# Moving two projection products, two reductions and an output gating in a fused attention and MLP kernel

## The chip, the cores and the metric

The kernel runs on one core of a Trainium2 chip. The metric is the device time of one execution in microseconds (us), as a median of several runs. A core has engines that run side by side, each through its own list of instructions in order: PE (TensorE, matrix products), DVE (VectorE), ACT (ScalarE), POOL (GpSimd) and SP (SyncE, which here issues most DMAs). They wait for one another by semaphores.

## What is computed

```python
x = A_x
xn = _layernorm(x, axis=-1)
s = _A_ref(xn, A_k_cache, A_v_cache, A_wq, A_wo)   # softmax attention, 32 heads of 128, 2048 queries, 2048 keys, then @ wo
g = _silu(_B_ref(xn, B_w1, B_w2, B_w3, B_w4))      # a token-shifted mixer and a gelu MLP of width 1792
return x + s * g
```

The model width is 512 and all tensors are bf16.

## The kernel before, in words

**Stages.** A first part computes the layer norms and the B branch up to the gate; what is left of the B branch runs beside the first units of attention. Attention is the main loop. A *unit* `u` is one head times 512 queries; there are 128, ordered by groups of four heads (`g`), query tile (`qt`), head (`hh`). A unit has eight *slots* (`SPU`), and `n` counts slots over the whole loop, `p` within the unit. In each slot PE makes two score matmuls (`s_slot`, tile `ps_s`, 128x512 each), ACT takes the exponential of both at once (L447, tile `pT`), and PE makes two probability times value matmuls (`pv_slot`, tile `ps_o`) for the slot ten back. The score tile has two buffers in PSUM, so a slot's score matmuls wait for the exponential of the slot two back.

**Sums of the softmax.** DVE and POOL add up a unit's exponentials: `add_first` (L453), `add_half` (L458, one half on POOL, one on DVE), `add_next` (L462). `fold` (L466) and `fold_last` (L470) halve the result twice. `turn` (L495) sends it through a DMA transpose into `tT`, issued by SP; `turned_sums` (L500) reduces it on DVE, a reciprocal follows, and two DMAs (`dr`, then `rb`, `bcast`, L512) spread it over the partitions. `norm` (L524) multiplies the unit's output by it into `oT`.

**Query projection.** For most units the queries of two heads at a time are made by a seven-product scheme (Strassen with shared sums): `product(v, k)`, k from 1 to 7, two matmuls of 128x256 each into `ps_q`; `q_take` (L416, ACT) and `q_part` (DVE: part 0 is L424, part 1 L427, part 2 L429, part 3 L432) add the products up. The sixteen slots of units v-2 and v-1 are the pair's schedule: product 1 in slot 0, 6 in 2, 2 in 5, 7 in 8, 5 in 9, 4 in 12 and 3 in 13. Parts 0 to 3 run in slots 2, 9, 9 and 14; the score matmuls of unit v start in slot 16 and read what part 3 writes.

**Output projection.** The product with `wo` has the same seven-product form in most (g, qt) blocks: `wo_product` (two matmuls of 128x256 into `ps_wo`), `wo_take` (L598, DVE, adds a product into the running output `sacc`), `o_sum` (L573, DVE, builds the sums of `oT` in the buffers so0 to so3, one buffer each). A block has two rounds `i` of sixteen slots; in round i product k stands in slots 10, 11, 14, 15, 19, 20 and 23 for k = 1, 7, 2, 4, 6, 5, 3, and takes in 12, 16, 22 and 24. `o_sum` 0 of the next block comes in slot 4 of that block, which is slot 20 of the last round of the one before, and it overwrites so0, which product 5 of that round reads. In the other blocks (the first and the last ones) plain matmuls of 128x512 are spread over the slots, each followed by an addition on DVE (L657, L664 or L668).

**The output.** For the first eight token tiles the last stage is `y_last`: a gating multiplication (L676), an addition of the residual (L678) and a DMA out. One tile becomes ready in each of the last units, in slot 7, and `y_last` runs in slot 3 of the next unit. For the other tiles the gate is applied ahead of time (`y_scale`, L636, and the residual by `y_add`, L640). The loads of the residual and the gate use a pool of six buffers.

**Order.** The order on each engine is that of the program: it is written out by hand, slot by slot, in the tables `steps`, `o_steps` and `o_early` and in the main loop at the end. All matmuls have the line of one helper, L112, so they are told apart by their tiles: `ps_s`, `ps_o`, `ps_q`, `ps_wo`.

Of the kernel before, what the change touches and what calls it, by code (L numbers as in the profile page):

```python
# [9 lines left out]
ALU = mybir.AluOpType  # L10
# [7 lines left out]
def kernel(  # L18
# [15 lines left out]
    nc = tc.nc  # L34
# [16 lines left out]
    HG = 4  # L51
# [10 lines left out]
    pin = tc.keep_in_program_order  # L62
# [48 lines left out]
    def mm(out, lhsT, rhs, start, stop, **kw):  # L111
# [9 lines left out]
        out=ident[:], in0=diag[:], scalar1=0.0, scalar2=None, op0=ALU.is_equal))  # L121
# [276 lines left out]
    def turned(v, ps):  # L398
        return ps.rearrange("d i (r j) -> d i j r", j=4) if v in TURN else ps.unsqueeze(2)

    def q_tile(v, pl, **kw):
        shape = [P, 4, 4, 64] if v in TURN else [P, 4, 1, 256]
        return pl.tile(shape if "bufs" not in kw else [P] + shape[2:], **kw)
# [14 lines left out]
    def q_part(v, i):  # L418
        s = sw[v]
        ps = turned(v, s["ps"][:])  # L420
        t = lambda: q_tile(v, pS, dtype=FP32, tag="tq", bufs=3, name="tq")
        if i == 0:
            s["u"] = t()
            pin(nc.vector.tensor_tensor(out=s["u"][:], in0=ps[:, 1], in1=s["m1"][:], op=ALU.add))  # L424
        elif i == 1:
            s["u3"] = t()
            pin(nc.vector.tensor_tensor(out=s["u3"][:], in0=ps[:, 0], in1=s["u"][:], op=ALU.add))  # L427
        elif i == 2:
            pin(nc.vector.tensor_tensor(out=s["q"][:, 3], in0=ps[:, 1], in1=s["u3"][:], op=ALU.add))  # L429
        else:  # L430
            u = s["u"][:].unsqueeze(1)
            pin(nc.vector.tensor_tensor(  # L432
                out=s["q"][:, 1:3], in0=ps, in1=u.to_broadcast([P, 2] + list(u.shape[2:])), op=ALU.add))
            del sw[v]
# [33 lines left out]
    def fold_last(u):  # L468
        a = st[u]["acc"]
        pin(nc.vector.tensor_tensor(out=a[:, 0, :], in0=a[:, 0, :], in1=a[:, 1, :], op=ALU.add))  # L470
# [56 lines left out]
    sacc = {}  # L527
# [8 lines left out]
    def halves(x):  # L536
        return x.rearrange("p (a c) -> p a c", a=2)
# [74 lines left out]
    wog, sp, tw, so, wo_ps, gin = {}, {}, {}, {}, {}, {}  # L612
# [56 lines left out]
        if g == NG - 1:  # L669
            last.append(t)  # L670

    pair, last = {}, deque()

    def y_last(t):
        xl, gl = fin.pop(t), gin[t]
        pin(nc.vector.scalar_tensor_tensor(  # L676
            out=halves(gl), in0=sacc[t], scalar=0.5, in1=halves(gl), op0=ALU.mult, op1=ALU.mult))
        pin(nc.vector.tensor_tensor(out=xl[:], in0=gl, in1=xl[:], op=ALU.add))  # L678
        pin(nc.sync.dma_start(out=out2d[t * P:(t + 1) * P, :], in_=xl[:]))

# [314 lines left out]
    for g in range(NG - 1):  # L995
        b = (g * QT + QT - 1) * HG
        for hh in range(HG):
            h = (g + 1) * HG + hh
# [32 lines left out]
    def pv_run(n):  # L1031
        while pv_at[0] <= n - LAG:
            pv_slot(*divmod(pv_at[0], SPU))
            pv_at[0] += 1
# [11 lines left out]
    def wo_slot(part, n, each=2, **kw):  # L1046
        gg, t = wo_todo[0]
        if part < HG // each:
            wo_mm(gg, t, tuple(range(part * each, (part + 1) * each)), **kw)
            return  # L1050
        wo_todo.popleft()
        wo_post(gg, t, n)
        if gg == NG - 1 and t % 4 < 3 and t + 1 not in fin and t // 4 not in LATE:
            fin_load(t + 1)
# [7 lines left out]
    first, third = {}, {}  # L1062
    for v in pairs:
        a = (v - 2) * SPU
        for k, n in ((1, 0), (6, 2), (2, 5), (7, 8), (5, 9), (4, 12), (3, 13)):
            steps[a + n].append((product, v, k))
        for i, n in enumerate((0, 5)):
            steps[a + n].append((q_take, v, i))
        steps[a + 14].append((q_part, v, 3))
        first[v - 2] = v  # L1070
        third[v - 1] = (v,)

    o_steps, o_early = defaultdict(list), defaultdict(list)
    for g, qt in BLOCK:
        u0 = ((g * QT + qt) * HG + 6) * SPU
        for i in range(2):
            a = u0 + 16 * i
            for k, n in ((1, 10), (7, 11), (2, 14), (4, 15), (6, 19), (5, 20), (3, 23)):
                steps[a + n].append((wo_product, g, qt, i, k))
            for k, n, which in ((7, 12, o_early), (4, 16, o_early), (5, 22, o_steps), (3, 24, o_early)):  # L1080
                which[a + n].append((wo_take, g, qt, i, k))
        for i, n, which in ((2, 3, o_steps), (0, 4, o_early), (1, 12, o_early), (3, 19, o_steps)):
            which[u0 + n].append((o_sum, g, qt, i))
# [11 lines left out]
    for i, u in enumerate((10, 11, 12, 13, 14, 16, 18, 20)):  # L1095
        n = (LATER + u) * SPU
        t = 4 * LATE[0] + i
# [22 lines left out]
    def run_all(plan, n):  # L1120
        for fn, *args in plan.get(n, ()):
            fn(*args)
# [1 line left out]
    for j, u in enumerate((2, 2, 3, 4, 4, 5, 5, 6, 9, 9, 9, 9, 11, 11, 17, 21)):  # L1124
        at(u * SPU + 3, lambda qt=(j // 4 - 1) % QT, i=j % 4: x_sum(qt, i))
    for h in range(2, H, 2):
        for i, u in enumerate((((-4, -4, -3, -3), (-2, -1, 0, 0))[h % HG // 2] if h >= HG else (8, 8, 9, 9))):
            o_early[(h // HG * QT * HG + u) * SPU + 4].append((w_sum, h, i))

    for v in range(1, NU):  # L1130
# [4 lines left out]
    for n in range(UB * SPU):  # L1135
        u, p = divmod(n, SPU)
        if p == 0 and wo_box and u not in PLAN:
            wo_slot(4, n, each=1)
        s_slot(u, p)
        pv_run(n)  # L1140
        for v, dcs in q_plan.get(n, ()):
            q_mm(v, dcs)
        run_steps(n, product)
        run_steps(n, wo_product)
        run_steps(n, q_take)
        if p == 0 and 1 <= u:
            if u - 2 in TURN:
                turned_sums(u - 2)
                turned_recip(u - 2)
            run_all(o_early, n)  # L1150
            if u not in third:
                add_last(u - 1)
        if p == 1 and u - 2 in TURN:
            bcast(u - 2)
        if p == fold_at(u) and 1 <= u:
            for v in third.get(u, ()):
                add_last(u - 1)
                q_part(v, 1)
                q_part(v, 2)
            fold(u - 1)  # L1160
            if u != UA and u not in first:
                fold_last(u - 1)
        if p == 2 and u in first:
            q_part(first[u], 0)
            fold_last(u - 1)
        if p == 3 and u - 1 in TURN:
            turn(u - 1)
        for part, tag in CATCH.get(n, ()):
            wo_slot(part, n, tag=tag)
        for v, k in ((u + 1, 3), (u + 2, 7)):  # L1170
            if p == k and "psq" in st.get(v, ()) and (k == 3) == (v > FIRST):
                q_copy(v)
        if u - 2 in TURN:
            norm_p, sum_p, wo_p, each = 7, 5, 3, 1
        else:
            norm_p, sum_p, wo_p, each = 4, 5, 4, 1
        at_wo = [wo_p + i for i in range(HG // each + 1)]
        if FIRST - 2 <= u < LAST:
            at_wo = ([1, 3, 4, 6, 7], [0, 2, 3, 6, 7])[u % 2]
        if p == norm_p and 2 <= u and not u - 2 in TURN:  # L1180
            norm_queue(u - 2)
        if p == sum_p and 1 <= u and u - 1 not in TURN:
            sums(u - 1)
        if p == sum_p + 1 and 1 <= u and u - 1 not in TURN:
            bcast(u - 1)
        if u == UA and p in (1, 2, 3):
            wo_slot(p - 1, n)
            if p == 3:
                fold_last(u - 1)
        for at_p, part in PLAN.get(u, ()):  # L1190
            if at_p == p:
                wo_slot(part, n, each=2)
        if p in at_wo and u not in PLAN and wo_todo and pS is not None and (p == at_wo[0] or wo_box):
            wo_slot(at_wo.index(p), n, each=each)
        if p == norm_p and u - 2 in TURN:
            norm_queue(u - 2)
        run_steps(n, q_part)
        if p == 4:
            run_all(o_early, n)
            add_first(u)  # L1200
        run_all(o_steps, n)
        if p == 3 and last:
            y_last(last.popleft())
        if p == 6:
            add_half(u, nc.gpsimd, LO) if u in APART else add_next(u, 2)
        pay()
        held_mm(n)
        for fn in todo.pop(n, ()):
            fn()
        if pS is None and not held:  # L1210
            right.close()
            pS = right.enter_context(pool("pS", side="right", reuse_waits="tile"))
            for tag, n in [("tw0", 2)] + [(x, 1) for x in ("tw1", "tw3", "so0", "so1", "so2", "so3")]:
                pS.tile([P, 2, D // 2], BF16, tag=tag, bufs=n, name="room")
            pS.tile([P, 2, 256], BF16, tag="xs", bufs=XS, name="room")
            pS.tile([P, 256], FP32, tag="tq", bufs=3, name="room")
# [3 lines left out]
    n = UB * SPU  # L1220
# [27 lines left out]
    def pv_to(k):  # L1248
# [29 lines left out]
        out=diag[:], in0=diag[:], scalar1=0.0, scalar2=None, op0=ALU.is_equal))  # L1278
# [98 lines left out]
```

## Time and profile before

| what | value |
|---|---|
| time, median of 3 runs | 1220.84 us (1220.69 to 1221.07) |
| the profiled execution's own time | 1223.74 us |
| span of the profile, first to last instruction | 1221.9 us |
| PE / ACT / DVE / POOL busy | 1208.6 / 1107.4 / 1090.2 / 299.5 us |
| granted TensorE clock | 1.00 |

The profile is of one execution. Busy time of PE is that of matmuls, which are pipelined: a 128x512 matmul is recorded as 0.38 us, and the next one starts 0.216 us after it. A row of the timeline gives the start, the length, engine, line, operation, the tiles, the shape, the count of merged instructions, and in brackets the engine's idle time before it with what ended it. Some matmul records are missing.

### The profile page before, as it was taken

To read this page: it belongs to the slowest core of one execution; us is meant where nothing else is said; L and a number is where in the kernel's file an instruction comes from. 1 tells how busy PE (TensorE), PEld (TensorE's weight loads), DVE (VectorE), ACT (ScalarE), POOL (GpSimd) and SP (SyncE) were. 2 spreads that over 40 slices of the span, in tenths; PEclk is the share of its full clock that TensorE was granted. 3 is DMA by queue.
4 is the path that set the end of the run, shared out by engine and by line. 5 is a ranking of instruction groups with operands and counts; after the bars stand their busy time and mean duration, and the time that the engine had idled before them with its cause. 6 is when DMAs were issued, how large, how long until landed. Compare 5 with 4: busy or idle time off the path is not lost.

```text
span 1221.9 us, 18835 instructions
## 1 busy us (share of the span) xinstructions
PE 1208.6 (99%) x6534; PEld 673.1 (55%) x6657; DVE 1090.2 (89%) x1931; ACT 1107.4 (91%) x1243; POOL 299.5 (25%) x222
## 2 busy tenths in 40 slices
PE   9999999999999999999999999999999999999998
PEld 6466444555555555555555555555555555555455
DVE  7863788999999989999999899999999999989997
ACT  6345999999999999999999999999999999999996
POOL 5300001323222222222222222222222222223320
PEclk9999999999999999999999999999999999999999
DMA  7672323434443434345345434343443534356642
GB/s 178 170 154 57 56 57 83 96 90 94 82 86 84 104 61 96 82 96 91 71 90 87 100 69 85 90 96 78 87 87 87 100 72 89 83 107 108 119 113 66
DMA packets 248159, 113.07 MB, mean 93 GB/s; under 512 B 195328, under 2 KB 231296, under 8 KB 248064
## 3 DMA queue, kind: packets, MB, share of 16 engines
q1 hardware_dynamic: 244560, 107.21, 42.2%
q0 software_dynamic: 2944, 4.20, 1.5%
q8 instruction: 52, 0.85, 0.3%
q14 instruction: 43, 0.35, 0.2%
q10 hardware_dynamic: 560, 0.46, 0.1%
HBM read 69.60 MB, written 4.45 MB: 61 GB/s over the span
## 4 chain that ended last, share of the span: by engine, by line
PE 85%; DVE 7%; DMA 5%; issue 1%; ACT 1%; DVEq 0%; POOL 0%
PE ps_s L112 36%; PE ps_o L112 32%; PE ps_q L112 7%; PE ps_wo L112 7%; PE ps_m L112 3%; DMA tT<-acc 2%; DMA rb<-dr 2%; DVE acc L462 1%; ACT pT L447 1%; DVE sm L500 1%; DMA dr<-rc 1%; DVE acc L453 1%; DVE acc L458 1%; DVE oT L524 0%; DVE acc L466 0%
## 5 line engine op out<-in xcount | busy, mean ns | idle before, releaser
L447 ACT ACTIVATE pT<-ps_s 128x1024 bf16<-128x1024 f32 x1016 | 1016.4, 1028 | 45.4 <-PE ps_s L112 14.3
L112 PE MATMUL ps_s<-qT,kT 128*128 128x512 bf16 (+1 forms) x2056 | 607.5, 377 | 1.0 <-DVE qT L432 0.7
L112 PE MATMUL ps_o<-pT,vb 128*128 128x512 bf16 x1884 | 568.3, 379 | 4.7
L458 POOL TENSOR_TENSOR acc<-acc,pT 128x1024 bf16<-128x1024 bf16 x117 | 248.7, 2126 | 726.6 <-DVE acc L453 448.8
L112 PEld LDWEIGHTS <-vb 128*128 128x128 bf16 x1984 | 194.0, 98 | 216.6
L112 PEld LDWEIGHTS <-kT 128*128 128x128 bf16 x2064 | 230.8, 113 | 73.0 <-DVE qT L432 2.4
L462 DVE TENSOR_TENSOR acc<-acc,pT 128x2048 bf16<-128x2048 bf16 x137 | 167.7, 1224 | 20.9 <-ACT pT L447 5.1
L453 DVE TENSOR_TENSOR acc<-pT 128x2048 bf16<-128x2048 bf16 x127 | 154.7, 1218 | 9.2 <-ACT pT L447 9.1
L598 DVE TENSOR_TENSOR sacc<-ps_wo,sacc 128x512 f32<-128x512 f32 x200 | 121.9, 609 | 3.4 <-PE ps_wo L112 1.8
L524 DVE TENSOR_TENSOR oT<-ps_o,rb 128x512 bf16<-128x512 f32 x127 | 86.5, 681 | 8.8 <-DMA rb<-dr 8.4
L500 DVE TENSOR_REDUCE sm<-tT 128x4 f32<-128x512 bf16 x124 | 83.9, 676 | 7.6 <-DMA tT<-acc 7.3
L466 DVE TENSOR_TENSOR acc<-acc 128x1024 bf16<-128x1024 bf16 x127 | 87.2, 687 | 2.4
L458 DVE TENSOR_TENSOR acc<-acc,pT 128x1024 bf16<-128x1024 bf16 x117 | 80.1, 684 | 0.0
L112 PEld LDWEIGHTS <-wc 128*128 128x128 bf16 x448 | 43.8, 98 | 53.3 <-issue 0.7
L112 PE MATMUL ps_wo<-wo_h,oT 128*128 128x256 bf16 (+1 forms) x294 | 70.7, 307 | 0.5
L112 PEld LDWEIGHTS <-oT 128*128 128x128 bf16 x428 | 41.6, 98 | 45.6
L112 PEld LDWEIGHTS <-so 128*128 128x128 bf16 x400 | 39.1, 98 | 48.2 <-issue 1.3
L112 PEld LDWEIGHTS <-wq_h 128*128 128x128 bf16 x396 | 38.7, 98 | 46.0
L112 PE MATMUL ps_q<-xnT,wq_h 128*128 128x256 bf16 (+1 forms) x281 | 58.2, 294 | 0.2
L301 ACT ACTIVATE h2T<-ps_s 128x1024 bf16<-128x1024 f32 x28 | 28.7, 1023 | 31.6 <-PE ps_s L112 31.6
L470 DVE TENSOR_TENSOR acc<-acc 128x512 bf16<-128x512 bf16 x127 | 53.4, 420 | 2.4
L112 PEld LDWEIGHTS <-w_sb 128*128 128x128 bf16 x368 | 33.5, 98 | 29.2
(134 smaller groups left out, 923.6 us busy)
## 6 DMA issues: line engine op xcount, KB each, us to landing
rb<-dr SPq DMA_DIRECT2D x127, 256.0 KB, 4.0
vb<-in_A_v_cache_dram SPq DMA_DIRECT2D x62, 256.0 KB, 3.0
wq_h<-in_A_wq_dram SPq DMA_DIRECT2D x32, 128.0 KB, 2.5
wo_h<-in_A_wo_dram SPq DMA_DIRECT2D x32, 128.0 KB, 2.6
w_sb<-in_B_w_dram SPq DMA_DIRECT2D x8, 256.0 KB, 4.9
kT<-in_A_k_cache_dram SPq DMA_TRANSPOSE x128, 2.7
gate<-xall POOLq DMA_DIRECT2D x16, 128.0 KB, 2.4
sacc<-in_A_x_dram POOLq DMA_DIRECT2D x8, 256.0 KB, 4.5
```

The costliest lines, as they stand in the source:

```text
L112: pin(nc.tensor.matmul(out=out, lhsT=lhsT, rhs=rhs, start=start, stop=stop, **kw))
L301: pin(nc.scalar.activation(out=h2[c][:, f], in_=ps[:], func=ACT.Gelu_apprx_tanh))
L447: pin(nc.scalar.activation(out=s["pT"][-1][:, jj:jj + 2, :], in_=sps[:], func=ACT.Exp, scale=SCALE))
L453: pin(nc.vector.tensor_tensor(out=s["acc"][:], in0=s["pT"][0][:], in1=s["pT"][1][:], op=ALU.add))
L458: pin(eng.tensor_tensor(out=a[:, part, :], in0=a[:, part, :], in1=e[:, part, :], op=ALU.add))
L462: pin(nc.vector.tensor_tensor(out=a[:], in0=a[:], in1=st[u]["pT"][i][:], op=ALU.add))
L466: pin(nc.vector.tensor_tensor(out=a[:, 0:2, :], in0=a[:, 0:2, :], in1=a[:, 2:4, :], op=ALU.add))
L470: pin(nc.vector.tensor_tensor(out=a[:, 0, :], in0=a[:, 0, :], in1=a[:, 1, :], op=ALU.add))
L500: pin(nc.vector.tensor_reduce(out=sm[:], in_=s["tT"][:], axis=mybir.AxisListType.X, op=ALU.add))
L524: pin(nc.vector.tensor_tensor(out=to, in0=o, in1=rb, op=ALU.mult))
L598: pin(nc.vector.tensor_tensor(out=out, in0=ps, in1=out, op=ALU.add))
```

## The change

It moves work within the hand-written order; nothing is added or left out of the computation.

1. The sixth and fifth output projection products go from slots 19 and 20 of their round to 18 and 19.
2. The fourth query product goes from slot 12 to slot 13 of its pair, where the third stands already.
3. In the first unit of a pair, `fold_last` goes ahead of `q_part` 0; in the second unit, `fold` and `fold_last` go ahead of `q_part` 2.
4. `y_last` loses its gating multiplication, which becomes `y_gate`. A tile that became ready before an odd unit is gated in slot 6 of it, and its addition and DMA follow in slot 3 of the next, even unit; in slot 3 of an even unit the tile that became ready just before is gated and finished as well.
5. One weight sum (`w_sum` 1) of the first head pair of the second group goes one unit later.

```diff
+    pair, last, gated = {}, deque(), []
+
+    def y_gate(t):
+        gl = gin[t]
+        pin(nc.vector.scalar_tensor_tensor(
+            out=halves(gl), in0=sacc[t], scalar=0.5, in1=halves(gl), op0=ALU.mult, op1=ALU.mult))
 
     def y_last(t):
         xl, gl = fin.pop(t), gin[t]
-        pin(nc.vector.scalar_tensor_tensor(
-            out=halves(gl), in0=sacc[t], scalar=0.5, in1=halves(gl), op0=ALU.mult, op1=ALU.mult))
         pin(nc.vector.tensor_tensor(out=xl[:], in0=gl, in1=xl[:], op=ALU.add))
...
-        for k, n in ((1, 0), (6, 2), (2, 5), (7, 8), (5, 9), (4, 12), (3, 13)):
+        for k, n in ((1, 0), (6, 2), (2, 5), (7, 8), (5, 9), (4, 13), (3, 13)):
             steps[a + n].append((product, v, k))
...
-            for k, n in ((1, 10), (7, 11), (2, 14), (4, 15), (6, 19), (5, 20), (3, 23)):
+            for k, n in ((1, 10), (7, 11), (2, 14), (4, 15), (6, 18), (5, 19), (3, 23)):
                 steps[a + n].append((wo_product, g, qt, i, k))
...
-        for i, u in enumerate((((-4, -4, -3, -3), (-2, -1, 0, 0))[h % HG // 2] if h >= HG else (8, 8, 9, 9))):
+        for i, u in enumerate((((-4, -4 if h > HG else -3, -3, -3), (-2, -1, 0, 0))[h % HG // 2] if h >= HG else (8, 8, 9, 9))):
...
             for v in third.get(u, ()):
                 add_last(u - 1)
                 q_part(v, 1)
-                q_part(v, 2)
             fold(u - 1)
             if u != UA and u not in first:
                 fold_last(u - 1)
+            for v in third.get(u, ()):
+                q_part(v, 2)
         if p == 2 and u in first:
+            fold_last(u - 1)
             q_part(first[u], 0)
-            fold_last(u - 1)
...
-        if p == 3 and last:
-            y_last(last.popleft())
+        if p == 3 and u % 2 == 0:
+            if gated:
+                y_last(gated.pop())
+            if last:
+                y_gate(last[0])
+                y_last(last.popleft())
+        if p == 6 and u % 2 and last:
+            y_gate(last[0])
+            gated.append(last.popleft())
```

More of the change, by code (lines that the diff above doesn't have):

```diff
@@ L670, in wo_post @@
             last.append(t)
-    pair, last = {}, deque()
+    pair, last, gated = {}, deque(), []
[3 more added lines that the diff above has]
+            out=halves(gl), in0=sacc[t], scalar=0.5, in1=halves(gl), op0=ALU.mult, op1=ALU.mult))
     def y_last(t):
         xl, gl = fin.pop(t), gin[t]
-        pin(nc.vector.scalar_tensor_tensor(
-            out=halves(gl), in0=sacc[t], scalar=0.5, in1=halves(gl), op0=ALU.mult, op1=ALU.mult))
         pin(nc.vector.tensor_tensor(out=xl[:], in0=gl, in1=xl[:], op=ALU.add))
```

## The prediction, made before the changed kernel ran

> **What bounds the kernel now.** First the page's head and busy times, then busy time by stretches: the main loop, and sixteen slots (one head pair) inside it.
>
> ```profile
> span 1221.9 us, 18835 instructions
> PE 1208.6 (99%) x6534; PEld 673.1 (55%) x6657; DVE 1090.2 (89%) x1931; ACT 1107.4 (91%) x1243; POOL 299.5 (25%) x222
> ```
>
> ```profile
> 128.00:1200.00 1072.00, 1064.49 (x5582) 584.49 (x5691) 992.37 (x1714) 1026.81 (x1124) 267.40 (x138) 1.00 0.43 88
> ```
>
> ```profile
> 447.28:464.15 16.87, 16.77 (x92) 9.45 (x93) 16.37 (x29) 16.34 (x20) 4.24 (x2) 1.00 0.35 72
> ```
>
> In the last two rows the columns are length, then busy time of PE, PEld, DVE, ACT and POOL. In the sixteen slots from 447.28 three engines look full, so busy time can't say which one sets the pace; counting can. A row of the chain of waits, from a stretch in which nothing but 512-wide matmuls ran, gives their spacing:
>
> ```profile
> 80.88 10.74 PE ps_s L112 x49
> ```
>
> The last of 49 adds its 0.38, so the spacing is (10.74 - 0.38) / 48 = 0.216 us. Two 256-wide ones take 0.22 together (rows at 459 below), 0.11 each. Sixteen slots hold 64 wide matmuls and 28 narrow ones: 64 x 0.216 + 28 x 0.11 = 13.82 + 3.08 = 16.9 us, the whole stretch. PE sets the pace there, and it can't be made shorter by an order. In the whole main loop PE is idle for 1072.00 - 1064.49 = 7.5 us, some of it holes of 0.05 us where a matmul record is missing. So **7.5 us is a ceiling**, and what can be won are PE's real stops. The timeline of PE, searched for matmuls that start over 0.2 us later than due, gives six (each pair of rows is before and after one):
>
> ```profile
> 232.76 0.59 PE L112 MATMUL ps_o<-pT,vb 128*128 128x512 bf16 x2
> 233.70 0.38 PE L112 MATMUL ps_wo<-wo_h,so 128*128 128x256 bf16 x2 [0.34 <-DVE sacc L598]
> ...
> 441.33 0.38 PE L112 MATMUL ps_o<-pT,vb 128*128 128x512 bf16 x1
> 441.92 0.38 PE L112 MATMUL ps_q<-xnT,wc 128*128 128x256 bf16 x2 [0.20 <-DVE qT L429]
> ...
> 445.16 0.38 PE L112 MATMUL ps_wo<-tw,oT 128*128 128x256 bf16 x2
> 445.65 0.62 PE L112 MATMUL ps_s<-qT,kT 128*128 128x512 bf16 x2
> ...
> 706.51 0.59 PE L112 MATMUL ps_o<-pT,vb 128*128 128x512 bf16 x2
> 707.47 0.38 PE L112 MATMUL ps_wo<-wo_h,so 128*128 128x256 bf16 x2 [0.36 <-DVE sacc L598]
> ...
> 1139.38 0.59 PE L112 MATMUL ps_o<-pT,vb 128*128 128x512 bf16 x2
> 1140.21 0.62 PE L112 MATMUL ps_s<-qT,kT 128*128 128x512 bf16 x2 [0.24 <-DVE qT L432]
> ...
> 1156.94 0.59 PE L112 MATMUL ps_o<-pT,vb 128*128 128x512 bf16 x2
> 1157.99 0.41 PE L112 MATMUL ps_s<-qT,kT 128*128 128x512 bf16 x1 [0.46 <-DVE qT L432]
> ```
>
> The loss is the second start less the first, less 0.216 per wide and 0.11 per narrow matmul between: 233.70 - 232.76 - 0.43 = 0.51; 441.92 - 441.33 - 0.22 = 0.37; 445.65 - 445.16 - 0.22 = 0.27; 0.53; 0.40; 0.62. **Together 2.70 us**, all waits for DVE: for a take (L598), for part 2 (L429), for part 3 (L432). So the question is only where DVE comes late, and whether the change makes it late elsewhere.
>
> **The change, part by part.**
>
> *Output products 6 and 5 a slot sooner.* The group view of DVE shows what that frees, the waits view what else DVE waits for:
>
> ```profile
> L573 DVE TENSOR_TENSOR so<-oT 128x512 bf16<-128x512 bf16 x50 | 20.9, 421 | 14.0 <-PE ps_wo L112 14.0
> ```
>
> ```profile
> DVE oT L524 <- DMA rb<-dr: 8.4, 15, 1.4
> DVE sm L500 <- DMA tT<-acc: 7.3, 16, 1.2
> ```
>
> `o_sum` 0 overwrites so0 in the very slot in which product 5 still reads it, and DVE stands for 14.0 us over the blocks. One slot sooner, all 14.0 us go. On PE that is worth nothing in itself, since none of the six stops follows such a wait closely; DVE then waits for `rb`, `tT` or ACT instead. I count 0 us (at most the stops it might still cover, none found). Product 6 now has to find take 4 done one slot sooner:
>
> ```profile
> 462.83 0.66 DVE L598 TENSOR_TENSOR sacc<-ps_wo,sacc 128x512 f32<-128x512 f32 x1
> ```
>
> ```profile
> 466.44 0.38 PE L112 MATMUL ps_wo<-tw,so 128*128 128x256 bf16 x2
> ```
>
> 466.44 - 463.49 = 2.95 us to spare, and a slot is at most 0.86 + 0.44 = 1.30 long: no stop.
>
> *PE's slots become uneven.* A slot without a product lasts 4 x 0.216 = 0.86 us, with one 1.08, with two 1.30. In block stages two such slots (1 and 6) become four (1, 4, 6, 12), and 2 and 13 hold two products. The work that hides this is ACT's:
>
> ```profile
> 447.54 1.95 ACT L447 ACTIVATE pT<-ps_s 128x1024 bf16<-128x1024 f32 x2
> ```
>
> ```profile
> 448.45 1.96 ACT L447 ACTIVATE pT<-ps_s 128x1024 bf16<-128x1024 f32 x2
> ```
>
> Exponentials can follow each other every 448.45 - 447.54 = 0.91 us, though one lasts 1.03. In slots 4 to 6, the worst run, ACT needs 3 x 0.91 and 0.26 for the query copy in slot 5, 2.99; PE takes 0.86 + 1.08 + 0.86 = 2.80. ACT falls 0.19 behind. A score matmul may start when the exponential of two slots back has ended: 0.59 + 1.03 = 1.62 after that slot's start, and the two slots last 1.94. So 0.32 is there and 0.19 is used: 0 us, 0.1 us a pair (5 us over 50 rounds) if that cover were 0.2 thinner.
>
> *`fold` and `fold_last` ahead of part 2, and product 4 a slot later.* The timeline of DVE and PE in slots 9 to 13 of a pair:
>
> ```profile
> 456.91 0.41 DVE L427 TENSOR_TENSOR tq<-ps_q,tq 128x256 f32<-128x256 f32 x1
> 457.36 0.42 DVE L429 TENSOR_TENSOR qT<-ps_q,tq 128x256 bf16<-128x256 f32 x1
> 457.70 0.68 DVE L466 TENSOR_TENSOR acc<-acc 128x1024 bf16<-128x1024 bf16 x1
> 458.42 0.43 DVE L470 TENSOR_TENSOR acc<-acc 128x512 bf16<-128x512 bf16 x1
> 458.76 0.68 DVE L598 TENSOR_TENSOR sacc<-ps_wo,sacc 128x512 f32<-128x512 f32 x1
> ```
>
> ```profile
> 459.08 0.38 PE L112 MATMUL ps_q<-xnT,wc 128*128 128x256 bf16 x2
> 459.30 0.59 PE L112 MATMUL ps_s<-qT,kT 128*128 128x512 bf16 x2
> ```
>
> `fold` and `fold_last` take 458.76 - 457.70 = 1.06 us of DVE, part 2 0.34. So `fold_last` ends 0.34 sooner and part 2 1.06 later. Product 4 waits for part 2 (the stop at 441.9 names L429, though it writes the side that only part 1 reads). It starts 459.08 - 457.78 = 1.30 after part 2 now. A slot later it starts only 0.86 later in block stages, because slot 12 is then empty. So its spare time shrinks by 1.06 - 0.86 = **0.20 us**, to 1.10; behind it on PE stand product 3 and the next scores. Product 3 and part 3 keep their times. In the first unit of a pair `fold_last` goes ahead by part 0's 0.34 likewise, and part 0 comes 0.42 later; product 2, its next waiter, is three slots behind. What is won is that each transpose is issued 0.34 sooner in both units, and with it the chain `tT`, sum, `rb`. SP's order doesn't change, so the K and V loads behind a transpose move with it.
>
> *Where that chain made DVE late:*
>
> ```profile
> 436.54 0.69 DVE L524 TENSOR_TENSOR oT<-ps_o,rb 128x512 bf16<-128x512 f32 x1 [1.40 <-DMA rb<-dr]
> 437.90 0.69 DVE L500 TENSOR_REDUCE sm<-tT 128x4 f32<-128x512 bf16 x1 [0.67 <-DMA tT<-acc]
> ```
>
> ```profile
> 699.10 0.69 DVE L524 TENSOR_TENSOR oT<-ps_o,rb 128x512 bf16<-128x512 f32 x1 [0.42 <-DMA rb<-dr]
> 700.19 0.69 DVE L500 TENSOR_REDUCE sm<-tT 128x4 f32<-128x512 bf16 x1 [0.40 <-DMA tT<-acc]
> ```
>
> At 437 DVE lost 2.07 us, and the two stops 441.9 and 445.65 follow. With `tT` 0.34 sooner DVE is 0.34 sooner: product 4 then stops 0.37 - 0.34 + 0.20 = 0.23, and the scores 0.27 - 0.34 + 0.14 (PE being that much sooner) = 0.07. Gain 0.64 - 0.30 = **0.34** (bounds 0 and 0.64). At 700 both waits shrink by up to 0.34, 0.68 in all, more than the stop: gain **0.53** (bounds 0 and 0.53).
>
> *One weight sum a unit later.* It stands right ahead of the first stop:
>
> ```profile
> 231.62 0.29 DVE L376 TENSOR_TENSOR wc<-wq_h,wc 128x256 bf16<-128x256 bf16 x1
> 231.83 1.22 DVE L453 TENSOR_TENSOR acc<-pT 128x2048 bf16<-128x2048 bf16 x1
> ```
>
> It is the second sum of the second group's first pair, in slot 4 of unit 12. It takes 0.21 of DVE's time there, so the take behind comes 0.21 sooner: **0.21** of the 0.51 (bounds 0 and 0.29). A unit later it stands ahead of a part 3 that no stop follows.
>
> *The gating split.*
>
> ```profile
> 1137.28 0.69 DVE L676 SCALAR_TENSOR_TENSOR gl<-sacc,gl 128x512 bf16<-128x512 f32 x1
> ...
> 1138.34 1.22 DVE L453 TENSOR_TENSOR acc<-pT 128x2048 bf16<-128x2048 bf16 x1
> 1139.48 0.68 DVE L432 TENSOR_TENSOR qT<-ps_q,tq 128x512 bf16<-128x512 f32 x1
> ```
>
> In an odd unit the gating and the addition hold 1138.34 - 1137.28 = 1.06 us between `fold_last` and part 3, for which the next scores wait. Both go behind part 3. The stop of 0.40 at 1140.21 is gone. For the one at 1157.99 the work between two part 3s is the same as before (what leaves one odd unit enters the even one), so DVE arrives 1.06 sooner and PE 0.40: 0.66 against a stop of 0.62, just enough. Gain **1.02** (bounds 0.4 and 1.02). In even units `add_first`, a take and `norm` come behind one more addition, 0.34 later; the sums of a unit take no time from PE until the scores, a unit on. SP issues two output DMAs in a row there, ahead of the next residual and gate loads, which need a buffer that the first of them frees; nothing on PE waits for those in the same unit. The last slots do the same eight gatings in total, so the end isn't later.
>
> **Sum:** 0.34 + 0.53 + 0.21 + 1.02 = 2.10 us. The profiled execution took 1223.74, so 1221.64; it stands 2.90 above the median, which I carry over: 1220.84 - 2.10 = **1218.7**. With the lower bounds (0.4 in all) it is 1220.4, with the upper ones (2.48) 1218.4, and with all 2.70 1218.1.
>
> **The rivals.**
>
> 1. *DVE's time comes back as waiting.* The 14.0 us and the earlier folds only move DVE to the same landings of `rb` and `tT`, which already cost 8.4 and 7.3 us. For it: the transposes' landing is shared with the K and V loads behind them. Against it: the two gating stops have no DMA ahead of them. Gain 0 to 0.5: 1220.3 to 1221.0.
> 2. *Product 4 becomes the wait (slower).* Place: slot 13 of the 56 pairs. It decides when part 2 is over 1.10 us later than in the quoted pair. The stop at 441.9 shows that such lateness happens, and an equally late pair would now lose 0.37 + 0.20 = 0.57. If the transposes, issued elsewhere among the loads, land late in nine more pairs, that is 5.1 us, net of the sum 3.0 lost: 1223.8. Against it: now one pair of 56 stops there by over 0.2.
> 3. *DVE or ACT is the bound.* Then the 14.0 us of DVE would be had in full: 1220.84 - 14.0 = 1206.8. Against it stands the count above, which fills the 16.87 us with matmuls alone. The Trainium skill (page "Perfetto Trace Analysis", section "Identifying the Most-Contended Engine") says that busy time of matmuls is no measure of headroom and that one should take the weight loads' share for TensorE and occupancy for the others; by it PE with 9.45 of 16.87 has room, and DVE and ACT at 16.3 would be the engines to relieve. The trace doesn't bear that out here, because the starts, not the lengths, fill the time.
>
> **Chances.** Forecast 0.66, rival 1 0.19, rival 2 0.12, rival 3 0.03. About 0.2% (2.4 us) is what a measurement of this kernel tells from no change. Of the forecast some 0.15 lies beyond a gain of 2.4 us, so faster is 0.15 + 0.03 = 0.18; same is 0.51 + 0.19 = 0.70; slower 0.12. The range goes from the ceiling of the stops with 0.3 to spare, 1217.8, over rival 1 to 1221.4.
>
> **What would show it.** Right: L573 no longer waits for `ps_wo`; L500 waits less for `tT`; no idle ahead of `ps_s` for L432 after 1130; PE idle in the main loop down from 7.5 to about 5.4 us. Wrong: `ps_q` waiting for L429 in several pairs (rival 2); PE idle for ACT in slot 8 (the uneven slots); PE idle unchanged (rival 1).

## The result, and the profile after

The changed kernel takes 1224.36 us (1224.13 to 1225.11) where the kernel before, measured beside it, takes 1221.26 (1220.69 to 1222.17): a ratio of **1.0026 (1.0016 to 1.0036)**, 3.1 us slower. The forecast was 2.1 us faster.

The page of the changed kernel's profile begins like this (its execution took 1224.93 us):

```profile
span 1223.1 us, 18833 instructions
PE 1209.4 (99%) x6535; PEld 674.4 (55%) x6657; DVE 1101.9 (90%) x1931; ACT 1098.9 (90%) x1243; POOL 299.1 (24%) x222
```

DVE is busy 11.7 us longer than before (1101.9 against 1090.2) with the same 1931 instructions. Not all of that comes from the gating split: e1 below, which puts the gating back, has 1096.9. To see in which stage the time went, one line of the view of two tiles is enough: the output products with `so` begin and end the block stage, and the scores `ps_s` go on to the end. For the kernel before and for the changed one (the two times are the first and the last start):

```profile
L112 PE MATMUL ps_wo<-wo_h,so x192: 269/273/273, 220.4 to 1061.8; 128*128 128x256 bf16 x192
...
L112 PE MATMUL ps_s<-qT,kT x2056: 272/379/408, 115.3 to 1208.8; 128*128 128x512 bf16 x184, 128*128 128x256 bf16 x3
```

```profile
L112 PE MATMUL ps_wo<-wo_h,so x192: 272/273/273, 220.5 to 1060.1; 128*128 128x256 bf16 x192
...
L112 PE MATMUL ps_s<-qT,kT x2056: 271/379/380, 115.4 to 1210.0; 128*128 128x512 bf16 x184, 128*128 128x256 bf16 x3
```

The block stage went from 1061.8 - 220.4 = 841.4 to 839.6 us. The late stage, from its end to the last scores, went from 1208.8 - 1061.8 = 147.0 to 149.9. So the loss is in the last 160 us, where the gating split, the folds and query product 4 are what differs. The timeline of DVE and of POOL there, in unit 119:

```profile
1136.35 0.69 DVE L432 TENSOR_TENSOR qT<-ps_q,tq 128x512 bf16<-128x512 f32 x1
1136.96 2.25 DVE L676 SCALAR_TENSOR_TENSOR gl<-sacc,gl 128x512 bf16<-128x512 f32 x1
1139.13 0.68 DVE L668 TENSOR_TENSOR sacc<-ps_wo,sacc 128x512 f32<-128x512 f32 x1
```

```profile
1136.55 2.11 POOL L458 TENSOR_TENSOR acc<-acc,pT 128x1024 bf16<-128x1024 bf16 x1 [3.89 <-ACT pT L447]
```

Part 3 (L432) is indeed sooner. But the gating behind it, 0.69 us before, is recorded with 2.25. POOL's half addition has begun 0.41 us ahead of it and ends at 1138.66; the gating ends at 1139.21, 0.55 later. The same happens in units 121 and 123, while the other five gatings last 0.66 to 0.69. DVE comes late, and PE pays. Its timeline after 1140:

```profile
1144.72 0.38 PE L112 MATMUL ps_q<-xnT,wq_h 128*128 128x256 bf16 x2 [0.20 <-DVE tq L424]
1148.45 0.38 PE L112 MATMUL ps_wo<-wo_h,oT 128*128 128x512 bf16 x1 [0.33 <-DVE sacc L668]
...
1163.15 0.38 PE L112 MATMUL ps_q<-xnT,wq_h 128*128 128x256 bf16 x2 [0.38 <-DVE tq L424]
1166.88 0.38 PE L112 MATMUL ps_wo<-wo_h,oT 128*128 128x512 bf16 x1 [0.33 <-DVE sacc L668]
...
1177.31 0.59 PE L112 MATMUL ps_o<-pT,vx 128*128 128x512 bf16 x2 [0.42 <-DVE oT L524]
...
1190.32 0.27 PE L112 MATMUL ps_sum<-ones_t,acc 128*128 128x1 bf16 x4 [0.77 <-DVE qT L341]
```

The stops for part 3 (L432) are gone, as forecast. In their place PE waits for part 0, for the takes, for the normalisation and for the sums: whatever stands behind the gating on DVE.

What DVE waits for in the changed kernel, from the waits view:

```profile
DVE sacc L598 <- PE ps_wo L112: 12.5, 55, 0.3
...
DVE sm L500 <- DMA tT<-acc: 3.3, 6, 0.8
...
DVE oT L524 <- DMA rb<-dr: 2.2, 6, 0.7
```

The 14.0 us ahead of L573 are gone, the waits for `tT` and `rb` fell from 7.3 and 8.4 us, and DVE now waits for PE at its takes (1.8 us before).

### The profile page after: what moved, and what is told of

It is laid out like the page before. It is cut to its first block, busy times and chain, and to the rows that moved or that the text cites. A ratio compares the mean times of both kernels' runs of the same rounds, so it can differ in the third digit from the quotient of the medians.

```text
span 1223.1 us, 18833 instructions
## 1 busy us (share of the span) xinstructions
PE 1209.4 (99%) x6535; PEld 674.4 (55%) x6657; DVE 1101.9 (90%) x1931; ACT 1098.9 (90%) x1243; POOL 299.1 (24%) x222
## 4 chain that ended last, share of the span: by engine, by line
PE 93%; DVE 5%; issue 1%; ACT 1%; DMA 0%; DVEq 0%; SPq 0%; ACTq 0%
PE ps_s L112 39%; PE ps_o L112 35%; PE ps_q L112 8%; PE ps_wo L112 7%; PE ps_m L112 3%; DVE acc L462 1%; DVE acc L453 1%; ACT pT L447 1%; PE ps_warm L112 0%; DVE acc L466 0%; DVE gl L676 0%; DVE oT L524 0%; DVE acc L458 0%; DVE sm L500 0%; PE ps_oh L112 0%
## 5 line engine op out<-in xcount | busy, mean ns | idle before, releaser
L598 DVE TENSOR_TENSOR sacc<-ps_wo,sacc 128x512 f32<-128x512 f32 x200 | 123.6, 618 | 15.3 <-PE ps_wo L112 12.5
```

What stands on the lines that cost most here:

```text
L598: pin(nc.vector.tensor_tensor(out=out, in0=ps, in1=out, op=ALU.add))
```

## The experiments

**Theory A**: the split puts three gatings beside POOL's addition, DVE stands until that has ended, and this is the whole loss. **Theory B**: the order alone is at fault, since even units now carry three operations of the output in one piece. **Theory C**: the moves of products and folds cost time, and the profile of before was of an unusual execution.

The table gives each kernel's ratio to the kernel before on the same chip, and from its profile the lengths of the block stage and the late stage, read as above, and the longest gating (L676).

| kernel | ratio (95% interval) | block stage | late stage | longest L676 |
|---|---|---|---|---|
| before, first profile | 1 | 841.4 | 147.0 | 0.69 |
| before again (f4) | one execution, 1222.15 us | 840.1 | 146.4 | 0.69 |
| changed | 1.0026 (1.0016 to 1.0036) | 839.6 | 149.9 | 2.29 |
| e1 gating put back | 0.9988 (0.9979 to 0.9997) | 839.7 | 146.4 | 0.68 |
| e2 gating split alone | 1.0028 (1.0019 to 1.0037) | 840.0 | 149.4 | 2.29 |
| e3 no POOL beside it | 0.9989 (0.9980 to 0.9998) | 839.7 | 146.1 | 0.68 |
| e4 two tiles in even units | 1.0000 (0.9991 to 1.0009) | 840.0 | 147.7 | 0.69 |
| f1 gating in slot 7 | 0.9997 (0.9988 to 1.0005) | 839.6 | 147.1 | 0.85 |
| f2 as e3, split to 123 | 0.9993 (0.9984 to 1.0001) | 839.9 | 146.6 | 0.68 |
| f3 gating back, no POOL | 0.9991 (0.9982 to 0.9999) | 839.9 | 146.4 | 0.68 |
| g1 one piece, odd slot 7 | 1.0005 (0.9996 to 1.0014) | 840.3 | 147.6 | 0.97 |
| g2 products alone | 0.9993 (0.9984 to 1.0002) | 839.9 | 145.8 | 0.69 |
| g3 folds and product 4 alone | 0.9995 (0.9986 to 1.0004) | 840.3 | 145.9 | 0.68 |

**e1, the gating put back.**

```diff
-        if p == 3 and u % 2 == 0:
-            if gated:
-                y_last(gated.pop())
-            if last:
-                y_gate(last[0])
-                y_last(last.popleft())
-        if p == 6 and u % 2 and last:
-            y_gate(last[0])
-            gated.append(last.popleft())
+        if p == 3 and last:
+            y_gate(last[0])
+            y_last(last.popleft())
```

> The changed kernel with the gating as before (one piece, in slot 3 of every unit). Theory A (the split puts three gatings on DVE beside POOL's half addition, where they last 2.27 us instead of 0.68, and all of the loss comes from that): the whole loss goes and the other edits' gain of the block stage stays, 1.5 to 2.0 us below the kernel before, about 1219.5 where before has 1221.3. Theory B (the order alone: three more operations in even units make DVE late): the same here. Theory C (the moves of products and folds cost in executions without a stop at 441 and 707, and the profile of before was an unusual one): still above before, 1222 or more.

1221.44 us against 1222.73, a ratio of 0.9988 (0.9979 to 0.9997). The whole loss goes. The gain is 1.3 us, a little less than the 1.5 to 2.0 that were expected. Theory C, which had it still above before, falls.

**e2, the split alone**, on the kernel before.

> The kernel before with the gating split alone. Theories A and B: the loss of the late stage alone, 2.5 to 3.5 us slower than before, about 1224.3; L676 at 2.2 to 2.3 us in units 119, 121 and 123. Theory C: within 1 us of before.

1226.06 against 1222.73, 1.0028 (1.0019 to 1.0037): the split alone makes the whole loss. The gating of unit 121 on DVE and the addition on POOL:

```profile
1155.40 2.29 DVE L676 SCALAR_TENSOR_TENSOR gl<-sacc,gl 128x512 bf16<-128x512 f32 x1
```

```profile
1155.02 2.11 POOL L458 TENSOR_TENSOR acc<-acc,pT 128x1024 bf16<-128x1024 bf16 x1 [4.03 <-ACT pT L447]
```

Again the gating ends 0.56 after POOL (1157.69 and 1157.13). Unit 123 has 2.29 as well. In unit 119 the gating lasts only 1.81, less than the 2.2 that was expected there, because it started later against POOL's addition; it too ends 0.55 after POOL (1139.26 and 1138.71):

```profile
1137.45 1.81 DVE L676 SCALAR_TENSOR_TENSOR gl<-sacc,gl 128x512 bf16<-128x512 f32 x1
```

```profile
1136.60 2.11 POOL L458 TENSOR_TENSOR acc<-acc,pT 128x1024 bf16<-128x1024 bf16 x1 [4.02 <-ACT pT L447]
```

**e3, no POOL addition beside the gating.** This is the run that parts A from B: the order of the gating stays, and DVE even gets more to do.

```diff
-    APART = range(2 * HG, NU - 3)
+    APART = [u for u in range(2 * HG, NU - 3) if u not in (119, 121, 123)]
```

> The changed kernel, but in units 119, 121 and 123 DVE makes the whole addition that POOL halves (one operation of 1.22 us instead of one of 0.68), so that no POOL addition runs beside the gating. Theory A: L676 is back at 0.68 us in all eight, DVE gains 2.27 - 0.68 - 0.54 = 1.05 us in each of three units, and of the 4.2 us of PE stops after 1140 some 1 to 2 us remain: 1221.5 to 1222.5. Theory B: DVE has 0.54 us more to do in each of these units, so it is 0 to 1.5 us slower than the changed kernel, 1224.4 to 1226; L676 stays where it was or the stops do.

1221.36 against 1222.73, 0.9989 (0.9980 to 0.9998). All eight gatings are short again (count, then shortest, median and longest in ns):

```profile
L676 DVE SCALAR_TENSOR_TENSOR gl<-sacc,gl x8: 659/680/684, 1137.1 to 1193.8; 128x512 bf16<-128x512 f32 x8
```

That is better than theory A had asked for (1 to 2 us of stops were expected to stay; PE's one named stop between 1140 and 1200 is of 0.17 us idle). Theory B, which wanted it no faster than the changed kernel, falls as the cause of the loss.

**f3, the control.** POOL's addition goes to DVE as in e3, with the gating put back as in e1.

> Control: the changed kernel with the gating as before, and POOL's addition on DVE in units 119, 121 and 123. If the gain of the kernel without POOL's addition came from that addition's place by itself and not from the gating beside it, this is faster than the gating put back alone (by 0.3 us or more). By theory A POOL's addition costs nothing where no gating meets it, and DVE gets 0.54 us more in each of three units: the stops near 1155 grow, 0 to 1.5 us slower than the gating put back alone, 1221.5 to 1223 where before has 1222.7.

0.9991 (0.9982 to 0.9999), level with e1. Where that addition runs is worth nothing by itself; it counts only beside a gating.

**f1, the gating a slot later**, a smaller dose: POOL's addition is nearly over when the gating starts.

```diff
-        if p == 6 and u % 2 and last:
+        if p == 7 and u % 2 and last:
```

> The changed kernel with the odd units' gating one slot later, in slot 7, behind the take L668 and the normalisation L524; POOL's half addition still runs when it starts. Theory A (DVE stands until POOL's addition has ended, then needs 0.55 us more): the gating starts some 1.2 us later than in the changed kernel against the same end of POOL's addition, so it lasts 0.9 to 1.2 us instead of 2.27, DVE wins 1.1 to 1.3 us in each of three units, and the time comes to 2 to 3.5 us below the changed kernel, about the kernel before or 1 us less. If the 2.27 us were a property of the operation in that place and not of POOL's end, it would stay near 2.3 us, and the time with it, 3 us above before.

0.9997 (0.9988 to 1.0005), where the changed kernel has 1.0026: some 3.5 us better. In unit 121 (DVE, then POOL):

```profile
1156.07 0.85 DVE L676 SCALAR_TENSOR_TENSOR gl<-sacc,gl 128x512 bf16<-128x512 f32 x1
```

```profile
1154.25 2.12 POOL L458 TENSOR_TENSOR acc<-acc,pT 128x1024 bf16<-128x1024 bf16 x1 [3.90 <-ACT pT L447]
```

The gating starts 0.30 us ahead of POOL's end (1156.37) and ends 0.55 behind it (1156.92). Started 1.7 us ahead of POOL's end the gating lasts 2.25 or 2.29, started 1.26 ahead (e2) 1.81, started 0.30 ahead 0.85: each time up to POOL's end and 0.55 more. In units 119 and 123 of f1 it starts after POOL's end and lasts 0.68. What keeps f1 from e1's time is a stop of PE at the sums near 1188 (0.83 us idle). It comes after 0.92 us in which DVE stands for `rb` in unit 123:

```profile
1173.58 0.69 DVE L524 TENSOR_TENSOR oT<-ps_o,rb 128x512 bf16<-128x512 f32 x1 [0.92 <-DMA rb<-dr]
```

**e4, two tiles in slot 3 of even units**, nothing in odd ones.

```diff
+        if p == 3 and u % 2 == 0:
+            while last:
+                y_gate(last[0])
+                y_last(last.popleft())
```

> The changed kernel, but nothing in odd units: two tiles are gated, added and sent out in slot 3 of each even unit (2.1 us of DVE in one piece, 0.6 us more in even units than the changed kernel has). No POOL addition runs there. Theory A: L676 at 0.68 us in all, PE's stops after 1140 below 1.5 us, 1219.5 to 1220.5. Theory B: even units are fuller than in the changed kernel, so no better than it, 1224 to 1226.

1.0000 (0.9991 to 1.0009): between the two theories. All gatings last 0.68, and the loss of the changed kernel is gone, but the late stage is 147.7 us, 1.3 over the 146.4 of e1. PE's timeline names the place, units 125 and 126:

```profile
1187.59 0.27 PE L112 MATMUL ps_sum<-ones_t,acc 128*128 128x1 bf16 x4 [0.72 <-DVE qT L341]
...
1200.99 0.38 PE L112 MATMUL ps_wo<-wo_h,oT 128*128 128x512 bf16 x1 [0.89 <-DVE tm L664]
```

The second stop is idle for only 0.17 to 0.21 us in e3, f1, f2 and g1, which gate one tile in unit 126, so there theory B holds in a small way. For the first one, two tiles in one piece aren't shown to be the cause: f1 and g1 stop as long at the sums (0.83 and 0.72 us) and gate one tile in unit 124. What the three have in common is that DVE stands for `rb` in unit 123 (0.69 us in e4, 0.92 in f1, 0.71 in g1). In e1 and e3, where a gating runs ahead of the normalisation in that unit, neither that wait nor the stop appears.

**f2, e3 with the last two tiles as before.**

```diff
-        if p == 3 and u % 2 == 0:
+        if p == 3 and (u % 2 == 0 or u > 123):
...
-        if p == 6 and u % 2 and last:
+        if p == 6 and u % 2 and u < 124 and last:
```

> The kernel without POOL's addition beside the gating, with the split only up to unit 123; the last two tiles are gated as before, in slot 3 of units 125 and 126. Aimed at the one stop of 0.33 us that is left near 1199 (the output product that waits for DVE behind two tiles in unit 126). If that stop comes from the two tiles in unit 126: 0.3 us less than without this edit, 1.3 to 2.0 us below before; if not, no difference or a new stop at the last fold.

0.9993 (0.9984 to 1.0001), no better than e3, and its late stage is 146.6 against 146.1. The stop it aimed at stays (0.21 us idle, near 1200): the aim was missed.

**g1, a try for a better version**: one piece again, in slot 3 of even units and slot 7 of odd ones up to 123 (`if p == (7 if u % 2 and u < 124 else 3) and last`).

> A try for a better version: the changed kernel, with gating, addition and output of a tile in one piece again, in slot 3 of even units and of units 125 and later, but in slot 7 of odd units up to 123, behind part 3, the take and the normalisation. By theory A the gating starts about when POOL's addition ends, so it lasts 0.68 to 0.9 us, part 3 is not held up, and even units carry one tile only: stops after 1130 of 0 to 0.5 us, 1.3 to 2.0 us below before. If DVE's order in even units (the sums behind the additional operations) is what counts, a stop at the sums of unit 124 near 1187 stays, as in the kernel with the gating alone moved to slot 7, and it is level with before.

1.0005 (0.9996 to 1.0014), level with before and worse than e1: the gain of 1.3 to 2.0 us that was expected by theory A is missed. The gatings beside POOL are short, as it asked (0.79 and 0.97 us), but the stop at the sums of unit 124 stays (0.72 us idle). Units 119 and 121 give the clearest rows on what POOL's addition holds up. First DVE, then POOL:

```profile
1138.24 0.69 DVE L668 TENSOR_TENSOR sacc<-ps_wo,sacc 128x512 f32<-128x512 f32 x1 [0.23 <-PE ps_wo L112]
...
1156.62 0.97 DVE L676 SCALAR_TENSOR_TENSOR gl<-sacc,gl 128x512 bf16<-128x512 f32 x1
```

```profile
1137.56 2.12 POOL L458 TENSOR_TENSOR acc<-acc,pT 128x1024 bf16<-128x1024 bf16 x1 [3.89 <-ACT pT L447]
...
1154.92 2.12 POOL L458 TENSOR_TENSOR acc<-acc,pT 128x1024 bf16<-128x1024 bf16 x1 [3.90 <-ACT pT L447]
```

The take L668, which reads one operand from PSUM (`ps_wo`) and one from SBUF, runs wholly inside POOL's addition and lasts its usual 0.69. The gating, which reads `sacc` and `gl`, both in SBUF, is held to 0.55 after POOL's end (1157.59 and 1157.04). The take is no exception: in the whole profile of the changed kernel no L598, which also reads `ps_wo` and `sacc`, lasts over 0.69 us.

**f4, the kernel before once more.**

> The kernel before, profiled once more. If the stops of the block stage at 441.9, 445.7 and 707.5 belong to the program, they stand here again; if they belonged to that one execution, they are gone or elsewhere, and the ceiling of 2.70 us was too high by up to 1.2 us. The two stops ahead of part 3 at 1140 and 1158, which have no DMA ahead of them, should stand in both.

The two lines of the tile views, as above:

```profile
L112 PE MATMUL ps_wo<-wo_h,so x192: 269/273/273, 220.6 to 1060.7; 128*128 128x256 bf16 x192
...
L112 PE MATMUL ps_s<-qT,kT x2064: 272/379/409, 115.4 to 1207.1; 128*128 128x512 bf16 x185, 128*128 128x256 bf16 x3
```

840.1 us where the first profile of the same kernel had 841.4, and e2, which is the same in this stage, has 840.0. The product that had stopped for 0.53 us at 707 now stands in an unbroken row (the starts are 0.21 and 0.22 us apart):

```profile
705.82 0.38 PE L112 MATMUL ps_o<-pT,vb 128*128 128x512 bf16 x1
706.03 0.38 PE L112 MATMUL ps_wo<-wo_h,so 128*128 128x256 bf16 x2
706.25 0.59 PE L112 MATMUL ps_s<-qT,kT 128*128 128x512 bf16 x2
```

Reckoned like the prediction's losses, nothing is left of the stops at 441.9 and 445.65 either, and 0.05 us of the one at 233.7. The two stops for part 3 do stand here again, but smaller: 0.29 us at 1138.90, where the first profile had 0.40, and here 1156.33 - 1155.57 - 0.43 = 0.33 instead of 0.62:

```profile
1155.57 0.59 PE L112 MATMUL ps_o<-pT,vb 128*128 128x512 bf16 x2
1156.33 0.62 PE L112 MATMUL ps_s<-qT,kT 128*128 128x512 bf16 x2 [0.17 <-DVE qT L432]
```

**g2 and g3, one part each** on the kernel before: g2 the two output products a slot sooner, g3 the folds and query product 4.

> The kernel before with output products 6 and 5 a slot sooner and nothing else. The prediction's step (the 14 us for which DVE waits ahead of L573 are worth nothing on PE) says within 0.5 us of before, with that wait gone. If DVE were the bound, 10 us and more faster. If the uneven slots made PE wait for ACT, 2 to 5 us slower, with stops in slots 5 to 8.

> The kernel before with the folds ahead of the query additions and the fourth query product a slot later, nothing else. The prediction's step says up to 0.9 us faster through sooner transposes; since the stops at 441 and 707 were those of one execution, 0 to 0.4 us faster. By rival 2 (product 4 waits for part 2) slower, by stops ahead of ps_q with xnT and wc in several pairs.

0.9993 (0.9984 to 1.0002) and 0.9995 (0.9986 to 1.0004): neither can be told from no change, and both block stages (839.9 and 840.3) lie with the kernel before's 840.0 and 840.1. In both late stages the stops for part 3 are missing, though the gating stands where it did: no scores there start over 0.06 us late.

## Why the prediction was wrong, step by step

**The gating split is the step that failed.** It reckoned what part 3 wins when the gating goes behind it, gave the gating its old 0.69 us in the new place, and bounded the gain by 0.4 and 1.02, with no reason that shut out a loss. In odd units the new place is beside POOL's half addition, and there it lasts up to 2.29 us: 1.6 us of DVE in each of three units. The late stage became 3.5 us longer than that of e1 (149.9 and 146.4) where 1.02 less had been forecast. The rule could be read in the profile of before: in unit 118 DVE's own half of the addition, which also reads two tiles from SBUF, lasts 0.89 instead of 0.68 beside POOL's half, and ends 0.55 after it (1134.15 and 1133.60); the same length stands at 1167.98 and 1184.71. First DVE, then POOL, in the kernel before:

```profile
1133.26 0.89 DVE L458 TENSOR_TENSOR acc<-acc,pT 128x1024 bf16<-128x1024 bf16 x1
```

```profile
1131.48 2.12 POOL L458 TENSOR_TENSOR acc<-acc,pT 128x1024 bf16<-128x1024 bf16 x1 [6.65 <-DVE acc L453]
```

The Trainium skill (page "SBUF — State Buffer", section "SBUF: two separate sides") says that DVE and GpSimd share one pair of ports as an exclusive lock: a DVE operation with two SBUF inputs and a GpSimd operation that reads SBUF shut each other out, and the second one waits for the whole of the first. The trace agrees for a DVE operation that comes second: it lasts to POOL's end plus 0.55 us, e3 takes that away, and L668 with one PSUM input doesn't have it. That POOL waits for a DVE operation that started first, no run here shows.

**The 1.02 that the split was to win was mis-sized as well.** It was taken from the two stops for part 3 in one execution. They come to 1.02 us in the first profile and 0.62 in f4, and g2 and g3, which don't move the gating, have neither; this is also why the late stages of g2 and g3 (145.8 and 145.9 us) are shorter than those of the kernel before (147.0 and 146.4). Against rival 1 the prediction said that these stops have no DMA ahead of them. In the profile of before the second one does. DVE stood for `rb` and for `tT` a unit sooner and then ran without a break up to part 3:

```profile
1149.31 0.69 DVE L524 TENSOR_TENSOR oT<-ps_o,rb 128x512 bf16<-128x512 f32 x1 [0.43 <-DMA rb<-dr]
1150.45 0.69 DVE L500 TENSOR_REDUCE sm<-tT 128x4 f32<-128x512 bf16 x1 [0.45 <-DMA tT<-acc]
```

With 0.88 us of such waits the stop is 0.62, with 0.46 (f4) it is 0.33, with none (g2) there is none; e1, with 0.77, has 0.42, but g3, with 0.44, has none. That the waits make the stop is read from these profiles; no run tests it.

**The sizes of the block stage's stops** came from one execution too. Of the 841.4 us, 1.3 belonged to that execution alone (840.1 and 840.0 in two others). The stop at 707 stands in no other profile, and those at 441.9 and 445.65 in none that leaves product 4 in its slot, so the 0.34 and the 0.53 had nothing regular to win. The stop at 233 does come back: in the five profiles without the moved weight sum it is 0.51, 0.05, 0.40, 0.39 and 0.65 us, in the eight with it 0.32 at most and under 0.15 in six. The 0.21 for that edit fits these, though they spread widely. The block stages agree: in the eight kernels with all these moves they lie between 839.6 and 840.3, on average 0.2 us below 840.0. e1 shows that the edits without the split together gain 1.3 us in 1222.7 (0.4 to 2.6 by the interval). That this is near the 1.08 of the sum without the gating is luck as far as the profiles show: 0.87 of the 1.08 was counted on the stops at 441.9, 445.65 and 707. Where the rest of e1's gain comes from stays open.

**The step on the output products held.** Their 14.0 us of DVE are gone and are worth nothing that can be measured on PE (g2). So rival 3, by which DVE or ACT is the bound, is out: it asked for 14 us. (The section of the Trainium skill that rival 3 quotes, "Identifying the Most-Contended Engine" of the page "Perfetto Trace Analysis", names the share of peak matrix work beside the weight loads' share as the measure for TensorE. Rival 3 went by the second alone, so the page does not by itself say that PE has room here.) Rival 1 is right that DVE's time comes back as waiting, but not at the landings of `rb` and `tT`: these waits are 4.2 and 5.6 us in e1 (8.4 and 7.3 in the first profile of before, 4.7 and 6.3 in f4). They come back at the takes (L598), which wait 10.7 us for PE in e1. The uneven slots cost nothing either: no named wait of PE for ACT appears, and g2 isn't slower.

**Product 4's thinner margin** (rival 2, the slower side) exists but didn't decide: the changed kernel has no PE wait for L429. In e4 one of these products starts 0.26 us late, at 442.06, and in g1 one pair names the wait, 0.50 us idle:

```profile
442.73 0.38 PE L112 MATMUL ps_q<-xnT,wc 128*128 128x256 bf16 x2 [0.50 <-DVE qT L429]
```

The result lies at rival 2's time, but for another reason than rival 2 gave.

**The statement that the sums of a unit take no time from PE** was wrong as well: the changed kernel, e2, e4, f1 and g1 each have a stop of 0.72 to 0.83 us idle at the sums of unit 124. Nor does the end stay as it was: the output product near 1200 waits in e3 (0.17 us idle), and in the kernel before it doesn't.

What stays open is whether the split could gain anything without POOL beside it: e3 and e1 are level.

## What to carry to other kernels

Before moving an operation to a new place on its engine, look at what the neighbouring engine runs at that moment, and give the operation the price that the trace shows beside that neighbour, not its mean. A bound of the gain needs a reason why it can't be below zero; a second profile of the same kernel shows which stops come back. Of the versions tried, the changed kernel with its gating put back (e1) is faster than the kernel before and the changed one, if only by 0.1% over the former; e3 and f3 are level with it.

## What the runs showed of the hardware

A DVE operation that waits for POOL is not shown as idle: the wait lies inside its recorded time, so the three gatings alone added 2.25 + 2.29 + 2.29 - 3 x 0.68 = 4.8 us to DVE's busy time, with no instruction added. Unexpected was how exact it is: in all nine gatings beside POOL (three each of the changed kernel and e2, one of f1, two of g1) the end lies 0.55 or 0.56 us behind POOL's, whatever the start. Why it is 0.55 and not the whole 0.68 that the gating takes alone, no run shows.
